# Attention on eight 64-by-32 tiles of the array, a batch at a time, and PReLU as one scaling and one maximum

## The chip, the core and the metric

The program runs on one core of one Trainium2 chip. Its engines work side by side: TensorE (PE; its weight loads are listed apart as PEld), VectorE (DVE), ScalarE (ACT), GpSimd (POOL) and SyncE (SP), whose queue issues the transfers between HBM and the on-chip memory SBUF. TensorE writes to PSUM, in banks of 128 partitions by 512 words. Each engine works through its own list in order. The metric is the time of one execution in microseconds (us); three runs of the kernel before took 1742.65, 1750.32 and 1750.9 us, median 1750.32.

## The reference, cut to what matters

Eight batches, eight heads, 576 tokens of 64 numbers. Attention runs twice through 32 packed rows p of each head, then come two layers over 4608 tokens:

```
p_packed = sm_attn(p, k, v)               # per head: 32 x 576 logits, softmax over 576
x = sm_attn(q, p_packed, p_packed)        # per head: 576 x 32 logits, softmax over 32
h = x @ w_in                              # 512 -> 2048
g = max(h, 0) + alpha * min(h, 0)         # alpha = rand(2048) * 0.3, one for each column
x1 = g @ w_out                            # 2048 -> 512
out = (silu(x1 @ w_gate) * (x1 @ w_val)) @ w_out2     # 512 -> 1536 -> 512
```

The weights arrive as 64-bit floats.

## The kernel before

**Stages.** The first layer runs as 256 units `it`: 16 halves of a batch (288 tokens) by 16 blocks of 128 columns. `h_unit` makes h in six matmuls: the second attention's weights, as a high part and a rest (`a2h`, `a2l`), meet p_packed @ w_in (`ppw`), which `pp_win` has made before, so x itself is never formed. Then PReLU makes `g`, ACT rounds it to `hi` (L773), POOL makes the rest `lo` (L775), and two units later (`LAG1 = 2`) `o_unit` adds twelve matmuls to four banks `acc`. h has two banks. The second layer (L946 on, 72 steps of `gv_step`) follows the last unit.

**Attention.** `quad(g)` handles four heads, two quads to a batch. The 32 packed rows of its four heads fill 128 partitions, and two heads share a matmul: p stands in a block layout with zeros (`pbd`, `ppbd`), so that a matmul uses all 128 rows of the array and 64 columns; a pair `pr` of such matmuls covers the quad. `logits` (L427) does this for both attentions (`s1` with k, `s2` with q), `pp_win` (L579) for p_packed @ w_in, four pieces j to a batch. These matmuls read 32-bit floats and leave two records each in the trace. All other large ones read the format fp32r and leave one.

**PReLU.** Up to unit 47 (`RELU`) ACT makes relu(h) and relu(-h) (L756, L757) and DVE joins them (L758). From unit 48 DVE makes alpha * min(h, 0) and adds max(h, 0) (L762, L765), both from PSUM.

**What sets the order.** `START` and `EARLY` place the steps of batches 0 and 1 (quads a to d) and the conversions of the 32 weight pieces (the word `1`: `convert`, which calls `widen`: four or five DVE instructions, and some of ACT and POOL) before or after a unit. `STEPS`, `GROUPS` and `PPW` do it for batches 2 to 7. From unit 40 to about 240 the weights of the second layer are converted in between (`columns2`, `product2`, `rows2`), and written to HBM over SP's queue. A scheduler that simulates the engines makes the final lists.

Of the kernel before, what the change touches and what calls it, by code (L numbers as in the profile page):

```python
# [17 lines left out]
P = 128  # L18
T = 384
WP = 4  # L20
LAG1 = 2
RELU = 48
# [4 lines left out]
LOADS = "b.v a.v 1 a.q 1 1 b.q"  # L27
START = """
    a.kt0 b.kt0 a.pt a.kt1 b.kt1 b.pt a.s1 a.et a.pp b.s1 a.ppt b.et b.qt0 a.qt0 b.pp b.qt1 a.qt1
    a.s20 b.ppt b.s20 a.a20 b.a20 1 1 1 1 1 w00 1 1  # L30
"""
EARLY = {
    (0, 0): "c.pd d.pd",
    (0, 1): "c.pt 1 b.s21 c.kt0 c.kt1",
    (1, 0): "c.s1",
    (1, 1): "d.kt0 d.pt 1 c.et d.qt0 c.pp",
    (2, 0): "c.qt0",
    (3, 0): "w01 d.qt1 a.s21",
    (3, 1): "c.ppt b.a21",
    (4, 1): "1 d.kt1 d.s1 a.a21 c.qt1",  # L40
    (5, 1): "1",
    (6, 1): "1 d.et",
    (7, 0): "d.pp",
    (7, 1): "1",
    (10, 1): "c.s2 d.ppt d.s2 w10",
    (11, 1): "1",
    (13, 0): "d.a2",
    (15, 0): "c.a2",
# [20 lines left out]
BEHIND = {"c.k": 3, "c.q": 4, "c.v": 5, "d.k": 5, "d.q": 6, "d.v": 9}  # L69
# [6 lines left out]
    p=0, k=0, v=2, kt0=0, pt=1, kt1=3.5, s1=3.5, q=0, et=4.5, pp=6.5, qt0=4, qt1=10.5, ppt=7,  # L76
    s2=11, a2=15,
)
GROUPS = (4, 9.5)
# [25 lines left out]
def tile_kernel(  # L105
# [20 lines left out]

    nc = tc.nc
# [7 lines left out]
    HQ = 4  # L135
# [5 lines left out]
    NQ = H // HQ  # L141
# [38 lines left out]
    def col_job(w, table, name, f):  # L180


        def parts():
            c = slice((f % WP) * P, (f % WP + 1) * P)
            return [t[:, :, c] for t in piece(table, f // WP, name)]

        return w[:, 2 * f * P : 2 * (f + 1) * P].rearrange("(c p) f -> p c f", p=P), parts

    def row_job(w, table, name, f):


        def parts():
            return [t[:, f % WP, :] for t in piece(table, f // WP, name)]

        return w[f * P : (f + 1) * P, :], parts
# [60 lines left out]
    def convert(n=1):  # L256

        for src, parts in queue[:n]:
# [17 lines left out]
    def vscratch(name):  # L276
        return vp.tile([P, HQ * M6 * D], U32, tag="v", name=name)

# [17 lines left out]
    pbd = sm.tile([P, P], F32, name="pbd")  # L296
    ppbd = [sm.tile([P, P], F32, name=f"ppbd{i}") for i in range(2)]
    for t in [pbd] + ppbd:
        nc.vector.memset(t, 0.0)
    al = sm.tile([P, NF1], F32, name="al")  # L300
    nal = sm.tile([P, NF1], F32, name="nal")
# [3 lines left out]
    def quad(g, ptags=("at",), natural=False, evac=nc.scalar):  # L305


        b, q2 = divmod(g, NQ)
        h0 = HQ * q2
        st = {"t": 0}  # L310
        wide = nc.gpsimd if g == 3 else nc.vector

        def pst(shape, name):
            tag = ptags[st["t"] % len(ptags)]
            st["t"] += 1
            return ps.tile(shape, F32, tag=tag, name=f"{name}_{g}", bufs=2)

        def alloc(name):
            return utile("u", [P, S], f"{name}_{g}")

        def copy(out, in_):

            if evac is nc.scalar:
                nc.scalar.activation(out=out, in_=in_, func=AF.Copy)
            else:
                evac.tensor_copy(out=out, in_=in_)

        def load_t(src, name, perm):
            tiles = []
            for pr in range(2):  # L330
                t = alloc(f"{name}{pr}")
                for hh in range(2):
                    s = src[b, h0 + 2 * pr + hh]
                    for e in range(2):
                        blk = 2 * hh + e
                        dst = t[32 * blk : 32 * blk + 32, :]
                        if perm:
                            nc.sync.dma_start(
                                out=dst.rearrange("p (m u i) -> p m u i", i=32, m=M6),
                                in_=s.rearrange(  # L340
                                    "(u j m) (e i) -> e j m u i", j=32, m=M6, i=32
                                )[e],
                            )
                        else:
                            nc.sync.dma_start(
                                out=dst.rearrange("p (t i) -> p t i", i=32),
                                in_=s.rearrange("(t j) (e i) -> e j t i", j=32, i=32)[e],
                            )
                tiles.append(t)
            return tiles  # L350

        def s_p():
            st["pb"] = pbd
            for h in range(HQ):
                nc.sync.dma_start(
                    out=pbd[32 * h : 32 * h + 32, (h % 2) * D : (h % 2) * D + D],
                    in_=p[b, h0 + h],
                )

        def s_p_dense(pd, pb):  # L360
            st["pb"] = pb
            for h in range(HQ):
                nc.gpsimd.tensor_copy(
                    out=pb[32 * h : 32 * h + 32, (h % 2) * D : (h % 2) * D + D],
                    in_=pd[32 * h : 32 * h + 32, :],
                )

        def load_n(src, name):

            if natural:  # L370
                t = wflat("B", f"{name}_{g}")
            else:
                t = vp.tile([P, HQ * M6 * D], F32, tag="v", name=f"{name}_{g}")
            t = t[:PB, : HQ * M6 * D].rearrange("p (h m d) -> p h m d", h=HQ, m=M6)
            nc.sync.dma_start(
                out=t.rearrange("p h m d -> p h (m d)"),
                in_=src[b, h0 : h0 + HQ].rearrange("h (p m) d -> p h (m d)", p=PB),
            )
            return t

        def s_v():
            st["v"] = load_n(v, "v")

        def s_k():
            st["kr"] = load_n(k, "k") if natural else load_t(k, "kr", True)

        def s_q():
            st["qr"] = load_n(q, "q") if natural else load_t(q, "qr", False)

        def s_kt(pr):  # L390
            t = alloc(f"kT{pr}")
            st.setdefault("kT", []).append(t)
            if not natural:
                nc.vector.transpose(out=t, in_=st["kr"][pr])
                return
            turn(t, st["kr"], pr, "kt", "q (i e p) -> q e i p")

        def turn(t, src, pr, name, order):

            for h in range(2):  # L400
                tp = pst([P, 512], f"{name}{pr}{h}")
                flat = src[:, 2 * pr + h].rearrange("p m d -> p (m d)")
                for i in range(M6 // 2):
                    nc.tensor.transpose(
                        tp[:, i * PB : (i + 1) * PB], flat[:, i * P : (i + 1) * P], ident[:PB, :PB]
                    )
                for e in range(2):
                    copy(
# [687 lines left out]
```

## Time and profile before

| | |
|---|---|
| median of three runs | 1750.32 us |
| profiled execution | 1746.27 us, its span 1744.5 us |
| busy share of the span | PE 95%, PEld 85%, DVE 58%, POOL 46%, ACT 35% |
| mean granted TensorE clock | 0.985 |
| chain that ended last | PE 79%, DVE 8%, DMA 4%, issue 3% |

How to read it: a busy time is that of an engine's instructions; matmuls overlap in their pipeline, so the step from one matmul's start to the next is what it costs. Three stretches differ: the start (to about 235 us), the rest of the first layer (to 881 us), and the second layer.

### The profile page before, as it was taken

The numbers are of one execution on the slowest core, as the hardware profiler recorded it, in microseconds if no ns is written. First come the engines' busy times: TensorE is split into PE (matmuls) and PEld (weight loads), VectorE is DVE, ScalarE is ACT, GpSimd is POOL, SyncE is SP. The second block draws the span as 40 slices with busy tenths as digits, with TensorE's granted clock in tenths as the row PEclk, the third lists the DMA queues.
The fourth block names the chain that finished last, engine by engine and source line by source line (L and its number), as shares of the span: only waits on it lengthen the run. The fifth ranks groups of instructions, "written<-read, shape, count | busy, mean of one in ns | idle before, by whom it ended". The sixth has DMA issues, their size and how long they took to land.

```text
span 1744.5 us, 27383 instructions
## 1 busy us (share of the span) xinstructions
PE 1664.1 (95%) x10048; PEld 1476.3 (85%) x10048; DVE 1011.9 (58%) x1875; ACT 611.4 (35%) x1384; POOL 807.9 (46%) x824
## 2 busy tenths in 40 slices
PE   5698899999999999999999999999999999999997
PEld 3477687978888798988999989989988998999997
DVE  6999867686777768675553363363354336334332
ACT  6765553433344344342222232232232223223222
POOL 3556755656555555533333443433433434433443
PEclk7799999999999999999999999999999999999999
DMA  9433365554545445431264464445455446445442
GB/s 237 123 97 107 113 181 155 145 133 135 152 131 152 127 129 145 120 113 57 80 243 167 169 203 165 169 165 204 169 185 184 157 145 226 161 145 193 172 169 79
DMA packets 227749, 266.03 MB, mean 153 GB/s; under 512 B 130848, under 2 KB 190240, under 8 KB 227616
## 3 DMA queue, kind: packets, MB, share of 16 engines
q1 hardware_dynamic: 227616, 264.30, 47.7%
q8 instruction: 79, 1.29, 0.3%
q14 instruction: 54, 0.44, 0.1%
HBM read 214.70 MB, written 49.55 MB: 151 GB/s over the span
## 4 chain that ended last, share of the span: by engine, by line
PE 79%; DVE 8%; DMA 4%; issue 3%; ACT 2%; POOL 2%; SPq 1%; ACTq 0%; DVEq 0%; POOLq 0%
PE acc L290 6%; PE acc L292 6%; PE acc L291 6%; PE o L291 6%; PE o L292 6%; PE o L290 5%; PE yb L290 4%; PE yb L291 4%; PE yb L292 4%; PE h L290 3%; PE h L292 3%; PE h L291 3%; PE vb L291 3%; PE xb L291 3%; PE vb L292 3%
## 5 line engine op out<-in xcount | busy, mean ns | idle before, releaser
L775 POOL TENSOR_TENSOR lo<-g,hi 128x288 fp32r<-128x288 f32 x256 | 222.3, 871 | 230.3 <-ACT hi L773 192.4
L979 POOL TENSOR_TENSOR s<-s,p 128x384 f32<-128x384 f32 x72 | 74.5, 1034 | 475.1 <-ACT s L978 475.1
L773 ACT ACTIVATE hi<-g 128x288 fp32r<-128x288 f32 x256 | 112.3, 441 | 240.9 <-DVE g L765 166.2
L940 DVE TENSOR_TENSOR u<-vb,u 128x384 f32<-128x384 f32 x144 | 80.2, 557 | 186.2 <-PE vb L292 185.9
L292 PE MATMUL o<-wp,ph 128*128 128x512 f32 x432 | 171.9, 398 | 0.0
L291 PE MATMUL o<-wp,ph 128*128 128x512 f32 x432 | 171.3, 396 | 0.0
L290 PE MATMUL h<-a2h,ppw 128*128 128x288 f32 x512 | 159.2, 311 | 10.9 <-DVE ppw L590 4.9
L290 PE MATMUL o<-wp,pl 128*128 128x512 f32 x432 | 168.5, 390 | 1.0 <-POOL pl L1001 1.0
L762 DVE TENSOR_SCALAR g<-h,al 128x288 f32<-128x288 f32 x208 | 105.5, 508 | 103.4 <-PE h L292 80.7
L940 DVE TENSOR_TENSOR u<-yb,p 128x384 f32<-128x384 f32 x144 | 79.4, 551 | 146.7 <-PE yb L292 146.7
L290 PE MATMUL yb<-ring,gv 128*128 128x384 f32 x432 | 146.0, 338 | 7.6 <-DVE u L940 7.2
L292 PE MATMUL h<-a2l,ppw 128*128 128x288 f32 x512 | 152.0, 297 | 0.0
L291 PE MATMUL h<-a2h,ppw 128*128 128x288 f32 x512 | 152.0, 297 | 0.0
L1001 POOL TENSOR_TENSOR pl<-s,ph 128x384 fp32r<-128x384 f32 x144 | 146.8, 1038 | 5.8 <-ACT ph L999 5.8
L292 PE MATMUL yb<-ring,gv 128*128 128x384 f32 x432 | 144.4, 334 | 0.0
L291 PE MATMUL yb<-ring,gv 128*128 128x384 f32 x432 | 144.4, 334 | 0.0
L978 ACT ACTIVATE s<-p 128x384 f32<-128x384 f32 x72 | 37.7, 524 | 287.7 <-DVE p L940 287.7
L290 PEld LDWEIGHTS h<-a2h,ppw 128*128 128x128 f32 x512 | 97.3, 190 | 41.5 <-DVE g L765 10.8
L999 ACT ACTIVATE ph<-s 128x384 fp32r<-128x384 f32 x144 | 75.7, 526 | 138.5 <-DVE s L983 116.7
L985 POOL TENSOR_TENSOR s<-s,u 128x384 f32<-128x384 f32 x72 | 102.4, 1423 | 5.5
L290 PE MATMUL xb<-ring,gv 128*128 128x384 f32 x288 | 97.2, 338 | 6.9 <-DVE u L940 6.9
L966 DVE TENSOR_TENSOR s<-xb,s 128x384 f32<-128x384 f32 x72 | 40.0, 556 | 106.2 <-ACT s L965 106.2
(176 smaller groups left out, 4685.3 us busy)
## 6 DMA issues: line engine op xcount, KB each, us to landing
gv<-wgvd SPq DMA_DIRECT2D x144, 896.0 KB, 6.3
wgvd<-cva SPq DMA_DIRECT2D x84, 256.0 KB, 2.7
cva<-in_moe_w_out_dram SPq DMA_DIRECT2D x28, 512.0 KB, 3.5
v<-in_v_dram SPq DMA_DIRECT2D x16, 576.0 KB, 6.0
out_dram<-os SPq DMA_DIRECT2D x12, 768.0 KB, 3.9
cva<-in_moe_w_in_dram SPq DMA_DIRECT2D x16, 512.0 KB, 3.7
kr<-in_k_dram SPq DMA_DIRECT2D x96, 72.0 KB, 2.7
qr<-in_q_dram SPq DMA_DIRECT2D x96, 72.0 KB, 2.4
```

The costliest lines, as they stand in the source:

```text
L290: nc.tensor.matmul(o, wlo, xhi, start=start, stop=False, **kw)
L291: nc.tensor.matmul(o, whi, xhi, start=False, stop=False, **kw)
L292: return nc.tensor.matmul(o, whi, xlo, start=False, stop=stop, **kw)
L762: nc.vector.tensor_scalar(out=g32, in0=hp, scalar1=0.0, scalar2=al[:, f : f + 1], op0=ALU.min, op1=ALU.mult)
L773: nc.scalar.activation(out=hi, in_=x, func=AF.Copy)
L775: nc.gpsimd.tensor_tensor(out=lo, in0=x, in1=f32(hi), op=ALU.subtract)
L940: nc.vector.tensor_tensor(out=out, in0=bank, in1=x, op=ALU.add)
L966: nc.vector.tensor_tensor(out=s1, in0=xb, in1=s1, op=ALU.mult)
L979: nc.gpsimd.tensor_tensor(out=s2, in0=s2, in1=p1, op=ALU.mult)
L985: nc.gpsimd.tensor_tensor(out=s2, in0=s2, in1=u3, op=ALU.mult)
L999: nc.scalar.activation(out=hi, in_=x, func=AF.Copy)
L1001: nc.gpsimd.tensor_tensor(out=lo, in0=x, in1=f32(hi), op=ALU.subtract)
```

## The change

A batch is now one step (`attention(b)`), with all eight heads in it. Head 2i+r uses rows 64r to 64r+63 of the array and columns 32i to 32i+31. The zeros go, and so do the block layouts. What was a pair of matmuls for each of two quads is one set of eight smaller ones (`heads8`), whose results lie in two banks. The products with v use four tiles of 32 columns and 64 moving columns instead of two of 64 and 128. For batches 0 and 1, k and q are turned by plain 32-bit matmuls instead of transposes, and copied out 128 partitions at once. The first logits are copied to SBUF by ACT before their maximum. PReLU becomes one ACT instruction and one of DVE; rows of w_out get the sign `sg` (1 for alpha up to 1) in one more ACT instruction for each piece. `START`, `EARLY`, `STEPS` and `BEHIND` are rewritten; `GROUPS` goes.

```
+    def heads8(out, lhs, rhs):
+        for i in range(HP):
+            for r in range(2):
+                rows, n = slice(64 * r, 64 * r + 64), slice(32 * i, 32 * i + 32)
+                nc.tensor.matmul(out[r][n], lhs[rows, n], rhs[i][rows], start=True, stop=True)
...
-            for pr in range(2):          # logits: one bank, two matmuls
-                nc.tensor.matmul(t[64 * pr : 64 * pr + 64, :HS], lhs[:, 64 * pr : 64 * pr + 64],
-                    rhs[pr][:, half * HS : (half + 1) * HS], start=True, stop=True)
+            t = [pst(f"{name}{half}{r}")[:, :HS] for r in range(2)]
+            heads8(t, lhs, [rhs[i][:, c] for i in range(HP)])
...
+            for half in range(2):        # s_s1
+                s1 = logits(st["pT"], st["kT"], half, "s1")
+                for r in range(2):
+                    nc.scalar.activation(
+                        out=e[r][:, half * HS : (half + 1) * HS], in_=s1[r], func=AF.Copy)
...
+            for m in range(M6):          # s_pp
+                for i in range(HP):
+                    c = (m % 4) * P + 32 * i
+                    nc.tensor.matmul(pp[32 * i : 32 * i + 32, :D],
+                        st["ET"][r][m // 4][:PB, c : c + 32], v_of(r, i, m),
+                        start=(m == 0), stop=(m == M6 - 1))
...
-        for q2 in range(NQ):             # pp_win
-            for pr in range(2):
-                nc.tensor.matmul(o[r, :], ppT[NQ * b + q2][:, r], w[:, 2 * q2 + pr, :], ...)
+        heads8(o, ppT[b], [w[:, i, :] for i in range(HP)])
...
-        if it < RELU:                    # h_unit
-            begun[it] = nc.scalar.activation(out=r, in_=hp, func=AF.Relu)
-            nc.scalar.activation(out=g32, in_=hp, func=AF.Relu, scale=-1.0)
-            nc.vector.scalar_tensor_tensor(out=g32, in0=g32, scalar=nal[:, f : f + 1], in1=r, ...)
-        else:
-            nc.vector.tensor_scalar(out=g32, in0=hp, scalar1=0.0, scalar2=al[:, f : f + 1], ...)
-            nc.vector.scalar_tensor_tensor(out=g32, in0=hp, scalar=0.0, in1=g32, ...)
+        begun[it] = nc.scalar.activation(out=m, in_=hp, func=AF.Copy, scale=sal[:, f : f + 1])
+        nc.vector.scalar_tensor_tensor(
+            out=g32, in0=hp, scalar=sg[:, f : f + 1], in1=m, op0=ALU.mult, op1=ALU.max)
...
+                nc.scalar.activation(out=full, in_=full, func=AF.Copy, scale=sg[:, f : f + 1])
...
+STEPS = dict(
+    p=4, k0=4, k1=4, kt0=4, k2=4, kt1=5, k3=5, kt2=6, kt3=7, v0=4, pt=5, s1=8, et0=9.5, et1=11,
...
```

Before, on TensorE at unit 122, where piece 0 of batch 4's product with w_in is made (`ppw_00` and `ppw_01` are the banks of the two quads; x2 is the pair of a quad):

```order
L291 MATMUL acc_112_5262<-hi_5421,wo1h 128x288
L292 MATMUL acc_112_5262<-lo_5423,wo1h 128x288
L586 MATMUL ppw_00_5696<-wi_124,ppT_4957 64x512 x2
L586 MATMUL ppw_01_5701<-wi_124,ppT_5180 64x512 x2
L290 MATMUL h_5519<-a2h_4052,ppw_2_4218 128x288
L291 MATMUL h_5519<-a2h_4052,ppw_2_4218 128x288
```

After the change, at the same unit (`ppw_00` and `ppw_01` are now the banks of r = 0 and 1):

```order
L288 MATMUL acc_112_5496<-hi_5653,wo1h 128x288
L289 MATMUL acc_112_5496<-lo_5655,wo1h 128x288
L306 MATMUL ppw_00_5930<-wi_115,ppT_5350 32x512 x4
L306 MATMUL ppw_01_5931<-wi_115,ppT_5350 32x512 x4
L287 MATMUL h_5747<-a2h_3_4315,ppw_2_4389 128x288
L288 MATMUL h_5747<-a2h_3_4315,ppw_2_4389 128x288
```

Four matmuls of 64 columns have become eight of 32, at the same place. Not everywhere do the eight stand together. Piece 2 of batch 5, after the change, on TensorE about unit 150:

```order
L288 MATMUL acc_144_6785<-hi_6800,wo0h 128x288
L289 MATMUL acc_144_6785<-lo_6802,wo0h 128x288
L306 MATMUL ppw_20_6956<-wi_1527,ppT_6639 32x512
L306 MATMUL ppw_21_6957<-wi_1527,ppT_6639 32x512
L287 MATMUL h_6895<-a2h_4_5598,ppw_1_6045 128x288
L288 MATMUL h_6895<-a2h_4_5598,ppw_1_6045 128x288
L289 MATMUL h_6895<-a2l_4_5599,ppw_1_6045 128x288
```

Here two of the eight stand alone; the other six come 36 matmuls later. On ScalarE, before, at units 120 to 123:

```order
L773 ACTIVATE hi_5461<-g_120_5458 128x288
L702 ACTIVATE cva_103<-cva_102 128x256
L562 ACTIVATE a2h_5469<-a_5471 128x576
L773 ACTIVATE hi_5500<-g_121_5497 128x288
L589 ACTIVATE ppw_0_5695<-ppw_00_5696 128x512
L589 ACTIVATE ppw_0_5695<-ppw_01_5701 128x512
L773 ACTIVATE hi_5529<-g_122_5526 128x288
L773 ACTIVATE hi_5567<-g_123_5564 128x288
```

And after, at units 122 and 123 (`m` is sal * h, read from PSUM; `cva` are second-layer weights, L688 is L702 of before):

```order
L576 ACTIVATE ppw_0_5929<-ppw_01_5931 128x512
L735 ACTIVATE m_5755<-h_5747,sal 128x288
L688 ACTIVATE cva_100<-cva_100 128x256
L735 ACTIVATE m_5794<-h_5786,sal 128x288
L746 ACTIVATE hi_5758<-g_122_5754 128x288
L688 ACTIVATE cva_100<-cva_100 128x256
L746 ACTIVATE hi_5797<-g_123_5793 128x288
```

The first reading of h, which was DVE's, now stands in ACT's list, among the weight conversions.

## Rows read from the trace of the kernel before

**Rows 1.** Windows of the three stretches: us, then each engine's busy us (instructions).

```profile
0.00:235.00 235.00, 186.77 (x1178) 144.87 (x1179) 203.88 (x337) 144.98 (x344) 142.56 (x142) 0.91 0.50 135
235.00:881.00 646.00, 637.17 (x4528) 557.60 (x4527) 455.46 (x925) 244.66 (x587) 332.80 (x383) 1.00 0.47 132
881.00:1744.00 863.00, 840.13 (x4347) 773.79 (x4345) 352.55 (x614) 221.76 (x454) 332.56 (x299) 0.99 0.48 173
```

**Rows 2.** The same view, one stretch of the start: PE, PEld, DVE, ACT, POOL.

```profile
100.00:150.00 50.00, 45.04 (x319) 38.00 (x319) 46.63 (x76) 31.14 (x77) 32.12 (x29) 1.00 0.40 108
```

**Rows 3.** Timeline of PE, both column tiles at work: start, us, instruction, count.

```profile
510.15 0.30 PE L292 MATMUL h<-a2l,ppw 128*128 128x288 f32 x1
510.38 1.19 PE L430 MATMUL s<-kT,pT 128*64 128x288 f32 x8
511.50 0.40 PE L290 MATMUL acc<-hi,wo0l 128*128 128x288 f32 x1
511.74 0.29 PE L291 MATMUL acc<-hi,wo0h 128*128 128x288 f32 x1
511.86 0.29 PE L290 MATMUL h<-a2h,ppw 128*128 128x288 f32 x1
```

**Rows 4.** Timeline of PE, two matmuls of one and the same column tile.

```profile
567.27 0.29 PE L290 MATMUL h<-a2h,ppw 128*128 128x288 f32 x1
567.49 1.19 PE L430 MATMUL s<-qT,ppT 128*64 128x288 f32 x4
568.61 0.40 PE L291 MATMUL h<-a2h,ppw 128*128 128x288 f32 x1
```

**Rows 5.** Chain in order of time: start, us, line, records.

```profile
581.89 1.01 PE ppw L586 x4
...
630.90 1.87 PE ppw L586 x8
636.03 1.46 PE pp L492 x24
642.89 0.64 PE s L430 x4
```

**Rows 6.** Groups by line and shape on PE, 235 to 881 us.

```profile
L586 PE MATMUL ppw<-wi,ppT 128*64 128x512 f32 x192 | 48.9, 608 | 0.6 <-DVE ppw L590 0.6
...
L430 PE MATMUL s<-qT,ppT 128*64 128x288 f32 x96 | 23.6, 420 | 0.1
```

**Rows 7.** Groups by line and shape on DVE, 0 to 220 us.

```profile
L758 DVE SCALAR_TENSOR_TENSOR g<-g,nal,r 128x288 f32<-128x288 f32 x39 | 33.4, 856 | 6.2 <-ACT g L757 6.0
...
L326 DVE COPY qT<-qt 64x288 f32<-64x288 f32 x8 | 5.4, 676 | 1.1 <-PE qt L404 0.9
...
L326 DVE COPY kT<-kt 64x288 f32<-64x288 f32 x8 | 3.6, 455 | 9.3 <-PE kt L404 9.2
```

**Rows 8.** PReLU lines one by one: count, shortest/median/longest ns, first and last start.

```profile
L758 DVE SCALAR_TENSOR_TENSOR g<-g,nal,r x48: 502/560/1573, 60.1 to 244.7; 128x288 f32<-128x288 f32 x48
...
L762 DVE TENSOR_SCALAR g<-h,al x208: 411/512/521, 248.3 to 879.9; 128x288 f32<-128x288 f32 x104
...
L765 DVE SCALAR_TENSOR_TENSOR g<-h,g x208: 410/456/460, 249.3 to 880.4; 128x288 f32<-128x288 f32 x104
...
L756 ACT ACTIVATE r<-h x48: 388/395/413, 57.4 to 243.9; 128x288 f32<-128x288 f32 x48
```

**Rows 9.** Timelines of DVE and of POOL near 74 us.

```profile
74.02 1.55 DVE L758 SCALAR_TENSOR_TENSOR g<-g,nal,r 128x288 f32<-128x288 f32 x1
...
73.85 1.41 POOL L252 TENSOR_TENSOR wi<-cva,cva 128x512 f32<-128x512 f32 x1 [2.10 <-DVE cva L242]
```

**Rows 10.** Waits, 250 to 880 us: who, for whom, us in total, times, longest.

```profile
ACT cva L702 <- DMA wgvd<-cva: 43.7, 31, 3.5
...
ACT cva L215 <- DMA cva<-in_moe_w_val_dram: 16.1, 10, 5.0
...
ACT cva L712 <- DMA wgvd<-cva: 13.1, 6, 3.8
...
PEld h L290 <- DVE g L765: 10.8, 14, 2.2
```

More of the change, by code (lines that the diff above doesn't have):

```diff
@@ L295, in tile_kernel @@
     make_identity(nc, ident)
[L296 to L299, printed above, removed]
+    ppd = [sm.tile([P, P], F32, name=f"ppd{i}") for i in range(2)]
     al = sm.tile([P, NF1], F32, name="al")
-    nal = sm.tile([P, NF1], F32, name="nal")
+    sg = sm.tile([P, NF1], F32, name="sg")
+    sal = sm.tile([P, NF1], F32, name="sal")
     spare = sm.tile([P, 1], F32, name="spare")
@@ L395, in s_kt @@
                 return
[L396 to L408, printed above, removed]
-                        t[D * h : D * h + D, :].rearrange(order, e=2, p=PB)[:, e],
-                        tp[D * e : D * e + D, :HS].rearrange("q (i p) -> q i p", p=PB),
-                    )
+            src = st[name][i // 2][:, 2 * (i % 2) : 2 * (i % 2) + 2]
@@ new lines, in s_turn @@
+            order = dict(k="q (m p) -> q m p", q="q (p m) -> q m p")[name]
+            for e in range(2):
+                tp = pst(f"{name}t{i}{e}")
+                for m in range(M6 // 2):
+                    for r in range(2):
+                        nc.tensor.matmul(
+                            tp[D * r : D * r + D, m * PB : (m + 1) * PB],
+                            src[:, r, 3 * e + m, :],
+                            ident[:PB, :PB],
+                            start=True,
+                            stop=True,
+                        )
+                out = t.rearrange(order, m=M6)[:, 3 * e : 3 * e + 3]
+                in_ = tp[:, :HS].rearrange("q (m p) -> q m p", m=M6 // 2)
+                if evac[i % 2] is nc.scalar:
+                    nc.scalar.activation(out=out, in_=in_, func=AF.Copy)
+                else:
+                    evac[i % 2].tensor_copy(out=out, in_=in_)
@@ L437, in logits @@
             return t
         def s_s1():
-            s1 = [logits(st["pT"], st["kT"], half, "s1") for half in range(2)]
-            mx = sm.tile([P, 4], F32, tag="mx", name=f"mx_{g}")
-            for half in range(2):
-                nc.vector.tensor_reduce(
-                    out=mx[:, half : half + 1], in_=s1[half][:, :HS], axis=AX.X, op=ALU.max
-                )
-            nc.vector.tensor_reduce(out=mx[:, 2:3], in_=mx[:, 0:2], axis=AX.X, op=ALU.max)
-            nc.vector.tensor_scalar_mul(mx[:, 3:4], mx[:, 2:3], -SCALE)
@@ L467, in s_s1 @@
-            nc.vector.reciprocal(out=sums[:, 3:4], in_=sums[:, 2:3])
+            if b == 1:
+                both = wflat("B", "E_1")
+                e = [both[:, r * S : (r + 1) * S] for r in range(2)]
+                both = wflat("B", "ET_1")
+                st["ET1"] = [both[:, r * 1024 : r * 1024 + 768] for r in range(2)]
+            else:
+                e = [alloc(f"E{r}") for r in range(2)]
+            for half in range(2):
+                s1 = logits(st["pT"], st["kT"], half, "s1")
+                for r in range(2):
+                    nc.scalar.activation(
+                        out=e[r][:, half * HS : (half + 1) * HS], in_=s1[r], func=AF.Copy
+                    )
@@ new lines, in s_s1 @@
+            mx = sm.tile([P, 4], F32, tag="mx", name=f"mx_{b}")
+            for r in range(2):
+                nc.vector.tensor_reduce(out=mx[:, r : r + 1], in_=e[r], axis=AX.X, op=ALU.max)
+            nc.vector.tensor_scalar_mul(mx[:, 2:4], mx[:, 0:2], -SCALE)
+            sums = sm.tile([P, 6], F32, tag="sums", name=f"sums_{b}", bufs=2)
+            for r in range(2):
+                nc.scalar.activation(
+                    out=e[r],
+                    in_=e[r],
+                    func=AF.Exp,
+                    bias=mx[:, 2 + r : 3 + r],
+                    scale=SCALE,
+                    accum_out=sums[:, r : r + 1],
+                )
@@ L515, in s_s2, with spans @@
+        def spans(halves):
             n = len(halves) * HS
             lo = halves[0] * HS
[L517 to L526 removed]
```

453 lines of the change are left out of this document (197 added, 256 removed).

## The prediction

> **What bounds the kernel now.** I read the windows first, then the timeline of TensorE, then groups, single lines and waits. The windows split the first layer in two. From 235 to 881 us PE is busy 637 of 646 us: whatever its matmuls give up there comes off the time, as long as no other engine is late. Up to 235 us PE is busy 187 us only, and DVE 204; between 100 and 150 us DVE is busy 46.6 of 50 us, ahead of PE (45.0), POOL and ACT [rows 1, 2]. There DVE's work sets the pace. The second layer, 863 us, holds none of the changed code.
>
> So two prices are wanted: a visit of TensorE to attention work, and DVE's work per unit.
>
> **What the tiles cost now.** In the timeline, matmuls of 288 columns in fp32r start 0.13 us apart (511.74, 511.86). Logits come at 510.38; the first matmul after them starts 1.12 us later, and the gaps on both sides (510.15 to 510.38, 511.50 to 511.74) are 0.10 and 0.11 us longer than 0.13 [rows 3]. That visit was four matmuls, two on each column tile, eight records. The visit at 567.49 takes 1.12 us too, with four records, two matmuls of one column tile alone [rows 4]. Half the work in the same time: the two column tiles run side by side, and what costs is the number of turns on the fullest tile, not of matmuls. From the chain: a visit with one pair of logits 0.64 us, with two 1.12, so a turn (one matmul on each tile) is 0.48 us; a pair of 512 columns 1.01 us, two 1.87, so a turn is 0.86; six turns of the product with v 1.46 us, 0.22 a turn [rows 3, 5]. What is left of each visit (0.64 - 0.48, and so on), with the two longer gaps, is 0.35 us: the price of leaving and regaining the full array.
>
> **The change on TensorE, 235 to 881 us.** I counted turns and visits in the two orders from unit 37 on.
> - p_packed @ w_in: before, 192 records are 48 pairs [rows 6]; with two that stand before 235 us, 50 turns by 0.86 = 43.0 us. After: 24 pieces would be 24 turns, but the order splits some (two, then six), and a part costs a whole turn: 39. Eight tiles start one behind the other; I add 0.05 us a turn. 39 x 0.91 = 35.5. Gain 7.5.
> - Logits: before 66 turns by 0.48 = 31.7. After 33, by 0.53 = 17.5. Gain 14.2.
> - Products with v: before 72 turns by 0.22 = 15.6. After 72 turns with 64 moving columns instead of 128 on four tiles. No row shows such a short one: between half (0.11, if columns set it) and the same (0.22). I take 0.125, near the half, since the 0.48 and 0.86 turns go with their columns (288 : 512); 9.0. Gain 6.6, bounds 0 and 7.7.
> - Visits: 87 of this kind become 84. Gain 1.
> - Transposes of p: 24 become 12, of 128 columns and one record each, so not above the 0.13 us of rows 3. Gain 1.
>
> Sum 30 us, bounds 24 and 31. It rests on one thing that no row shows: that four column tiles by two row tiles run side by side like two column tiles do.
>
> The Trainium skill ("TensorE: Matmul & The Clock Gate", Measured speedup vs the span model) speaks against full credit: it states 2.38 for three tiles and 6.32 for nine, about 0.7 of ideal at nine. At 0.7 a turn of logits would be about 0.69 us and one of 512 columns 1.23, and the sum 18 us less, an estimate from that page. With two tiles, rows 3 and 4 show no such loss.
>
> **The change on DVE, up to 235 us.** L758 joins the two halves of PReLU from SBUF: 39 times by 220 us, 856 ns on average, 33.4 us [rows 7]. Its times are of two kinds, 502 at best, 560 in the middle, 1573 at worst [rows 8]. At 74.02 one takes 1.55 us while POOL runs an addition from 73.85 to 75.26 [rows 9]. L765, which reads PSUM and one tile of SBUF, has 410 to 460 ns in 208 cases, L762 at most 521 [rows 8], beside POOL work of 333 in 646 us [rows 1]. The new instruction has L765's form, so 0.46. Gain 39 x (0.856 - 0.456) = 15.6 us.
> The Trainium skill ("SBUF — State Buffer", two separate sides) names the cause: a port pair that DVE, with two SBUF inputs, and GpSimd lock in turn. The trace agrees in the 1.55 us; by it POOL gains too, of which I count nothing.
> The copies L326 (5.4 + 3.6 us [rows 7]) become 8 of 128 partitions at the same length, gain 4.5; maxima and sums in fewer, longer instructions, about 2. Together 22 us of DVE's work. Against it: PE's turning of batches 0 and 1 becomes plain matmuls of two records, some 8 us more (96 pairs of 96 columns, 0.48 x 96/288 = 0.16 us each, in place of 96 transposes of a single record, which I take at half); the first chain (k, logits, copies, exp, products) must now carry eight heads before anything of the second attention starts; sixteen pieces get one more ACT instruction; and the order puts more conversions ahead of unit 0. When DVE gives up 22 us, PE (187 of 235 us busy, at a mean granted clock of 0.91 [rows 1]) is close behind it. I count 12 of the 22; bounds +3 (nothing won, the longer chain shows) and -24.
>
> **After unit 48** DVE drops one instruction of 0.51 us for each of 208 units, ACT gains one of about 0.40 (L756's price [rows 8]), some 83 us on 245 busy of 646 [rows 1]. Neither engine bounds there. But m now stands in ACT's list behind conversions that wait for transfers: 43.7, 16.1 and 13.1 us of such waits, 5.0 us the longest [rows 10]. Until now h's bank was freed by DVE, which had no such waits. From the end of h's matmuls to the next use of the bank lie about 4 us (two units of 18 matmuls by 0.13 less h's own 0.8); m, g and two handovers need 1. A wait under 3 us costs nothing. The bounds are -11 (the 10.8 us that weight loads waited for g go [rows 10]) and +73 (every wait on a transfer reaches PE); I take 3, near the lower end, since the waits of the largest group average 1.4 us.
>
> **Sum.** 1746.3 (the profiled execution, 1744.5 of it the span) - 30 - 12 + 3 = 1707. That execution stands 4 us under the median of the runs shown, 1750.3, and 3.6 over the lowest; I leave 1707.
>
> **Rivals.**
> 1. *Eight tiles side by side are slower than two*: their operands come from more places at once, and each turn costs a third more. The 72 turns are 17.5 + 35.5 = 53 us, a third is 18: 1725. For it: rows 3 have two tiles, none has eight; against it: two cost no more than one [rows 3, 4]. 0.15. (The page named above would have it so.)
> 2. *Row tiles do not run side by side*, only column tiles do: each set of eight is two turns. 33 + 39 sets get a second one, 17.5 + 35.5 = 53 us: PE gives back all and 23 more; with the start's 12 won the time is about 1760. Nothing in this trace uses two row tiles. 0.05.
> 3. *ACT's list becomes the wait.* m queues behind transfers, h's bank comes free late, PE stands. In all, waits on transfers are some 73 us; more than half of it (42 us) must reach PE to eat the gain, which needs waits mostly over 3 us, while the group of 31 averages 1.4. In full: 1707 + 70 = 1777; in part (20 us) 1727. 0.10, of which 0.02 for slower than before.
> 4. *The start gives everything*, 24 us or more, because POOL too is freed of the lock: 1695. 0.20.
> 5. *The start gives nothing*, since transfers and the first chain set it, not DVE: 1719 to 1722. 0.10.
> My forecast keeps 0.40.
>
> **How the numbers follow.** Rivals 1, 4, 5 and the mild form of 3 lie at 1695 to 1727; with the bounds of the forecast (1707 - 14, 1707 + 18) and the 4 us between execution and median, the range is 1684 to 1736. A difference below 0.5% (9 us) can't be told from none. Faster by more than that, under 1741: all but rival 2, the hard end of 3 and some of 1 with 5 together, 0.88. Same 0.07, slower 0.05.
>
> **What would show it.** The changed profile should have logits visits of eight matmuls at about 0.7 us from first start to the next full matmul, and 512-column ones at about 1.1, where now a pair takes 0.64 and 1.01. If 1.1 and 1.9 stand there, rival 2 holds. The product with v: 12 turns in about 0.8 to 0.9 us a visit. The new DVE instruction: below 0.5 us everywhere, without the 1.5 us kind. Unit 40 should start some 12 us earlier, the second layer some 40 us earlier, and last the same 863 us. The forecast is wrong if PE's idle time before h, with ACT's m as its releaser, grows past 10 us, or if the start is no shorter.

## The result, and the profile after

The changed kernel takes 1772.28 us (median of 4 runs), the kernel before 1748.93 beside it: ratio 1.0145, interval [1.0125, 1.0164]. Forecast were 1707 us, in 1684 to 1736. It is slower by 1.45%, and the forecast is wrong in its sign.

Where it goes is read from windows cut at the same work: the first matmul of h of unit 40, and that of unit 255. Columns as in [rows 1]; the last three are granted clock, DMA share and GB/s. The kernel before:

```profile
0.00:219.70 219.70, 171.83 (x1058) 131.01 (x1059) 193.23 (x314) 133.93 (x312) 130.30 (x128) 0.91 0.49 136
219.70:878.80 659.10, 649.91 (x4632) 569.26 (x4630) 465.14 (x945) 255.44 (x619) 344.25 (x396) 1.00 0.47 131
878.80:1744.50 865.70, 842.33 (x4364) 776.00 (x4362) 353.52 (x616) 222.03 (x455) 333.36 (x300) 0.99 0.48 173
```

The changed kernel:

```profile
0.00:240.20 240.20, 176.76 (x1574) 138.67 (x1574) 174.89 (x288) 118.60 (x250) 127.33 (x111) 0.80 0.48 127
240.20:904.00 663.80, 628.10 (x5286) 549.88 (x5283) 383.26 (x683) 328.65 (x768) 346.03 (x395) 0.99 0.47 129
904.00:1774.00 870.00, 844.61 (x4364) 778.68 (x4362) 352.30 (x615) 222.54 (x456) 332.74 (x300) 0.99 0.48 173
```

Unit 40 starts 20.5 us later, where I forecast 12 earlier. The middle stretch is 4.7 us longer, where I forecast 27 shorter: TensorE's busy time did fall there, by 21.8 us, but its idle time rose from 9.2 to 35.7. The second layer is 4.3 us longer here; over the runs below, which leave it alone, it takes 860.3 to 873.0 us. The two profiled executions lie 29.5 us apart and the medians 23.4: the profile of the changed kernel is its slowest run.

The tiles themselves do what they should. TensorE's timeline of the changed kernel (start, us, instruction, records) has a whole set of logits, a part of a set of 512 columns, a whole such set, and a product with v:

```profile
452.62 0.71 PE L306 MATMUL s<-kT,pT 64*32 64x288 f32 x16
453.26 0.40 PE L287 MATMUL acc<-hi,wo1l 128*128 128x288 f32 x1
...
627.80 1.04 PE L306 MATMUL ppw<-wi,ppT 64*32 64x512 f32 x2
628.77 0.40 PE L287 MATMUL h<-a2h,ppw 128*128 128x288 f32 x1
...
661.43 1.09 PE L306 MATMUL ppw<-wi,ppT 64*32 64x512 f32 x16
662.45 0.40 PE L288 MATMUL acc<-hi,wo2h 128*128 128x288 f32 x1
...
478.43 0.88 PE L470 MATMUL pp<-v,ET 96*32 96x64 f32 x48 [1.50 <-DMA v<-in_v_dram]
```

Eight matmuls of 288 columns take 0.64 us to the next full matmul (0.65 in most sets), where one pair took 0.64 before [rows 5]; eight of 512 take 1.02 (a pair 1.01 before [rows 5]). One matmul of such a set alone takes 0.97. The last line has a wait that the kernel before did not have.

The costliest group of the new PReLU on each of DVE and ACT (busy, mean ns | idle before, what ended it), where before stood [rows 7, 8]:

```profile
L738 DVE SCALAR_TENSOR_TENSOR g<-h,sg,m 128x288 f32<-128x288 f32 x256 | 129.3, 508 | 172.9 <-ACT m L735 160.1
...
L735 ACT ACTIVATE m<-h,sal 128x288 f32<-128x288 f32 x256 | 125.3, 494 | 64.8 <-PE h L289 64.6
```

DVE's instruction is 0.51 us (0.46 forecast) and never over 0.52, m 0.49 (0.40 forecast). And the waits from 240 to 904 us (who, for whom: us in total, times, longest), as [rows 10]:

```profile
DVE g L738 <- ACT m L735: 146.4, 87, 4.3
...
PEld h L287 <- DVE g L738: 27.2, 32, 2.0
DVE qT L372 <- DMA qr<-in_q_dram: 25.4, 16, 3.7
...
PEld acc L289 <- POOL lo L748: 11.6, 21, 1.2
...
PE h L287 <- DVE g L738: 9.1, 13, 1.7
...
PE pp L470 <- DMA v<-in_v_dram: 8.5, 5, 3.4
```

Weight loads of h wait 27.2 us for g, not 10.8 [rows 10]. The forecast had named two signs against it. PE's idle time before h with m as its releaser did not pass 10 us: it is 9.1 us, and the releaser is g, though g in its turn waits 146.4 us for m. The other sign is there: the start is no shorter. The waits for transfers of q and of v are new too: the kernel before has none on v there, and 1.3 us on q.

To add TensorE up, I took every matmul's time to the next one's start, between units 40 and 255. Matmuls of the attention: 111.8 us before, 89.8 after, so 22.0 saved of the 30 forecast. The 3870 full-array matmuls, the same number in both: 547.3 us before, 574.0 after, so 26.7 more. The second number eats the first. Sorted by what comes next on TensorE, 13.1 of the 26.7 stand right ahead of attention matmuls (v's 8.5 us among them), 11.0 ahead of matmuls of acc, and 3.1 ahead of those of h.

### The profile page after: what moved, and what is told of

Same layout as the page of the kernel before. It is cut to its first block, busy times and chain, and to the rows that moved or that the text cites. A ratio compares the mean times of both kernels' runs of the same rounds, so it can differ in the third digit from the quotient of the medians.

```text
span 1774.0 us, 29492 instructions
## 1 busy us (share of the span) xinstructions
PE 1649.5 (93%) x11216; PEld 1467.2 (83%) x11216; DVE 910.5 (51%) x1585; ACT 669.8 (38%) x1472; POOL 806.1 (45%) x806
## 4 chain that ended last, share of the span: by engine, by line
PE 61%; issue 9%; POOL 9%; DMA 9%; DVE 8%; ACT 2%; SPq 2%; POOLq 0%; DVEq 0%; ACTq 0%
PE o L288 5%; PE o L289 5%; PE o L287 5%; PE yb L287 4%; PE yb L289 4%; PE yb L288 4%; POOL lo L748 3%; PE acc L289 3%; PE acc L287 3%; PE acc L288 3%; DMA wgvd<-cva 3%; PE vb L288 3%; PE xb L288 3%; PE vb L289 3%; PE vb L287 3%
## 5 line engine op out<-in xcount | busy, mean ns | idle before, releaser
L738 DVE SCALAR_TENSOR_TENSOR g<-h,sg,m 128x288 f32<-128x288 f32 x256 | 129.3, 508 | 172.9 <-ACT m L735 160.1
L287 PE MATMUL h<-a2h,ppw 128*128 128x288 f32 x512 | 161.7, 316 | 24.8 <-DVE g L738 17.4
L913 DVE TENSOR_TENSOR u<-vb,u 128x384 f32<-128x384 f32 x144 | 80.2, 557 | 187.2 <-PE vb L289 187.0
L288 PE MATMUL h<-a2h,ppw 128*128 128x288 f32 x512 | 154.1, 301 | 0.0
L735 ACT ACTIVATE m<-h,sal 128x288 f32<-128x288 f32 x256 | 125.3, 494 | 64.8 <-PE h L289 64.6
L289 PEld LDWEIGHTS h<-a2l,ppw 128*128 128x128 f32 x512 | 98.6, 193 | 7.8 <-issue 4.8
```

Of the source, the lines that this page charges most:

```text
L287: nc.tensor.matmul(o, wlo, xhi, start=start, stop=False, **kw)
L288: nc.tensor.matmul(o, whi, xhi, start=False, stop=False, **kw)
L289: return nc.tensor.matmul(o, whi, xlo, start=False, stop=stop, **kw)
L735: begun[it] = nc.scalar.activation(out=m, in_=hp, func=AF.Copy, scale=sal[:, f : f + 1])
L738: nc.vector.scalar_tensor_tensor(out=g32, in0=hp, scalar=sg[:, f : f + 1], in1=m, op0=ALU.mult, op1=ALU.max)
L913: nc.vector.tensor_tensor(out=out, in0=bank, in1=x, op=ALU.add)
```

## The experiments

All times are medians; each ratio is to the kernel before in the same session. "Unit 40" is its start, "40 to 255" the stretch between these two starts, both from the profiled execution.

| run | us | ratio, interval | unit 40 | 40 to 255 |
|---|---|---|---|---|
| before | 1748.93 | | 219.7 | 659.1 |
| after | 1772.28 | 1.0145 [1.0125, 1.0164] | 240.2 | 663.8 |
| e1 tiles, old PReLU | 1800.21 | 1.0305 [1.0282, 1.0329] | 257.5 | 672.8 |
| e2 new PReLU alone | 1749.23 | 1.0009 [0.9997, 1.0022] | 217.5 | 657.6 |
| e3 tiles from batch 2, old PReLU | 1771.22 | 1.0124 [1.0098, 1.0151] | 222.2 | 676.5 |
| e4 start reordered | 1775.23 | 1.0153 [1.0134, 1.0171] | 236.0 | 663.9 |
| e5 later use | 1780.17 | 1.0165 [1.0134, 1.0195] | 244.2 | 671.2 |
| e6 tiles from batch 2, new PReLU | 1763.81 | 1.0079 [1.0063, 1.0095] | 217.9 | 673.9 |
| e7 e6 with later use | 1760.65 | 1.0067 [1.0049, 1.0085] | 218.8 | 669.5 |
| e8 before, late q | 1750.00 | 1.0010 [0.9996, 1.0025] | 222.2 | 657.0 |
| e9 one v | 1773.10 | 1.0151 [1.0120, 1.0182] | 236.3 | 662.5 |
| e10 no q loads | 1760.11 | 1.0081 [1.0054, 1.0107] | 240.2 | 658.1 |
| e11 both | 1756.40 | 1.0058 [1.0038, 1.0078] | 241.1 | 650.8 |
| e12 spread loads | 1763.66 | 1.0104 [1.0078, 1.0129] | 238.2 | 654.3 |
| e13 e12, whole sets | 1788.37 | 1.0232 [1.0213, 1.0250] | 245.7 | 672.3 |
| e14 e12, third unit | 1755.55 | 1.0048 [1.0030, 1.0067] | 238.6 | 644.7 |
| e15 e6, spread, whole sets | 1762.30 | 1.0093 [1.0060, 1.0125] | 215.9 | 674.5 |
| e16 e2, less TensorE work | 1732.42 | 0.9916 [0.9899, 0.9932] | 216.1 | 641.9 |
| e17 e6, spread, third unit | 1744.31 | 0.9970 [0.9956, 0.9984] | 225.0 | 652.7 |
| e18 e2, third unit | 1751.45 | 1.0016 [1.0005, 1.0027] | 220.9 | 660.8 |

**The two halves of the change, apart: e1, e2, e3.** My first theory was that m in ACT's list had eaten the tiles' gain (theory A).

```diff
 # e1 on the changed kernel; e2 is the reverse, on the kernel before; e3: `if b < 2` old attention, else tiles
-        m = gp.tile(...); nc.scalar.activation(out=m, in_=hp, func=AF.Copy, scale=sal[:, f : f + 1])
-        nc.vector.scalar_tensor_tensor(out=g32, in0=hp, scalar=sg[:, f : f + 1], in1=m, op0=ALU.mult, op1=ALU.max)
+        if it < RELU: ...   # ACT twice, DVE once
+        else: ...           # DVE twice
```

> The changed kernel with the PReLU of before (ACT's two steps up to unit 47, two DVE instructions after it; w_out not scaled, no sg). Theory A: in the changed kernel m stands in ACT's list behind work that waits, g waits for m, and h's bank comes free late; that ate the 30 us which the tiles save. Then units 40 to 255 take 664 - 28 = about 636 us here, weight loads of h wait for g under 15 us (61 us of idle there in the changed kernel), and the time is about 1742. Rival B: the attention itself lost them (late transfers of v and q, more copies on ACT); then units 40 to 255 still take 655 to 665 us and the time is 1765 to 1772. The start stays late in both: unit 40 at 235 to 240 us.

> The kernel before with the new PReLU alone (m on ACT, one DVE instruction, rows of w_out scaled by ACT), attention untouched. Theory A: units 40 to 255 grow from 659 to about 680 us, with DVE's g waiting for ACT's m and h's weight loads for g; the start gains a few us at most; time 1760 to 1772. Rival B: the new PReLU costs nothing on the old attention; units 40 to 255 stay at 659, the start gains up to 12 us; time 1738 to 1750.

> The kernel before with its own start (batches 0 and 1 in the old attention) and its own PReLU; eight tiles only for batches 2 to 7. Theory A: the tiles give their 24 to 30 us when the PReLU is left as it was: units 40 to 255 take about 632 us, unit 40 starts where it did before (220 us), time about 1720. Rival B: the tiled attention brings waits of its own (v and q transfers, its longer chain): units 40 to 255 take 645 to 660 us, time 1735 to 1748.

Theory A falls on all three. The new PReLU alone changes nothing (1.0009), though DVE's g waits 161 us for m in that run too. With the tiles, the old PReLU is 28 us slower than the new one, 17 of them before unit 40. And tiles alone lengthen the middle stretch by 17 us (e3). Both e1 and e3 are worse than rival B had them, too. So the loss sits with the tiled attention, and the new PReLU softens it. DVE's groups up to unit 40, in the changed kernel, in e1 and in e2:

```profile
L738 DVE SCALAR_TENSOR_TENSOR g<-h,sg,m 128x288 f32<-128x288 f32 x39 | 19.5, 505 | 14.8 <-ACT m L735 11.8 <-POOL cva L689 2.7 <-POOL wi L248 0.2
```

```profile
L733 DVE SCALAR_TENSOR_TENSOR g<-g,nal,r 128x288 f32<-128x288 f32 x39 | 30.3, 778 | 16.5 <-ACT g L732 16.4
```

```profile
L765 DVE SCALAR_TENSOR_TENSOR g<-h,sg,m 128x288 f32<-128x288 f32 x39 | 19.7, 506 | 10.2 <-ACT m L762 6.3 <-POOL lo L775 2.1 <-POOL cva L710 1.8
```

The instruction fell from 856 ns [rows 7] to 506 in e2 as forecast, 13.7 us in 39 units; unit 40 came 2.2 us earlier (unit 0 starts 1.9 us later, units 0 to 39 take 4.1 us less). Little of DVE's time was what the old start waited for.

**The start: e4, e6.**

```diff
 # e4 on the changed kernel; in START three conversions move behind the first logits
-LOADS = "a.v0 a.v1 1", "a.q0 1 1 a.q1"
+LOADS = "a.v0 a.v1 a.q0 a.q1"      # alpha's load ahead of them; conversions 0 to 2 held behind the first Exp
 # e6: the kernel before up to batch 1, with the new PReLU; attention(b) and pp_win on tiles for b >= 2
```

> The changed kernel with its start in another order: alpha and q are loaded ahead of the first weights, and the first three conversions and sg are held until the maximum and the Exp of the first attention. Theory C: the first chain was late because kT's and E's copies stood behind conversions that wait for transfers; then unit 0 starts at about 68 us (80 in the changed kernel), unit 40 some 8 to 12 us earlier (about 230), time about 1762. Rival D: conversions set unit 40 whatever the chain does; unit 0 moves by a few us, unit 40 stays at 238 to 245, time 1770 to 1776.

> The start and the first two batches of the kernel before, eight tiles for batches 2 to 7 only, and the new PReLU. If the start's loss and the loss after unit 40 are separate sums, unit 40 starts near 217 us as with the new PReLU alone, units 40 to 255 take about 664 us as in the changed kernel, and the time is about 1750. Rival: the late start of the changed kernel is also what delays the later units (weight pieces converted later); then units 40 to 255 take 640 us or less, time about 1725.

The changed kernel's longest waits of TensorE up to 240 us, and the chain followed back from 82 us, by line:

```profile
PE et L456 <- ACT E L438: 13.8, 2, 10.7
PE h L287 <- DVE g L738: 8.3, 6, 2.5
PE h L287 <- ACT a2h L543: 7.3, 1, 7.3
...
by line: DMA cva<-in_moe_w_in_dram 18.8%; issue 9.9%; DMA cva<-in_moe_w_out_dram 9.1%; SPq L349 9.0%; DMA k<-in_k_dram 6.3%; DVE cva L231 5.7%; DVE cva L238 4.0%; DVE cvb L212 3.9%; DVE cva L223 3.0%; DVE cvb L223 2.9%; POOL cva L236 2.6%; 
```

The first chain carries eight heads and stands in ACT's and DVE's lists between conversions that wait for weights. Unit 0 starts at 80.2 us instead of 50.9. All of the start's loss lies before it: units 0 to 39 take 160.0 us, 8.8 less than before. With the chain put first (e4) unit 0 starts at 71.4, but unit 40 gains only 4 us and the time nothing: the first seven pieces of w_out came 5 to 11 us later instead. With the old start (e6) unit 40 is back at 217.9. So the start's 20 us belong to the first two batches on tiles, with the order that was written for them. The middle stretch of e6, though, takes 673.9 us and not 664, so the time is 1764 and not the 1750 expected; its TensorE visits to p_packed @ w_in take 52.5 us instead of 45.2. Why, I could not settle; the order of its instructions differs.

**Transfers of q and v: e5, e7, e8.** In eight rotating buffers now stand the tiles of eight heads, and v's two halves share one buffer. The changed kernel's timeline shows q's transfers and v's second half issued in one stretch, and DVE and TensorE waiting:

```profile
471.30 1.91 SPq L336 DMA_DIRECT2D qr<-in_q_dram  x2
472.03 0.78 DVE L372 STREAM_TRANSPOSE qT<-qr 128x576 f32<-128x576 f32 x1 [0.28 <-DMA qr<-in_q_dram]
...
473.31 0.44 SPq L349 DMA_DIRECT2D v<-in_v_dram  x1
473.80 5.33 SPq L336 DMA_DIRECT2D qr<-in_q_dram  x7
474.34 0.78 DVE L372 STREAM_TRANSPOSE qT<-qr 128x576 f32<-128x576 f32 x1 [1.53 <-DMA qr<-in_q_dram]
475.04 0.48 DVE L738 SCALAR_TENSOR_TENSOR g<-h,sg,m 128x288 f32<-128x288 f32 x1
...
479.54 0.78 DVE L372 STREAM_TRANSPOSE qT<-qr 128x576 f32<-128x576 f32 x1 [2.52 <-DMA qr<-in_q_dram]
480.24 0.48 DVE L738 SCALAR_TENSOR_TENSOR g<-h,sg,m 128x288 f32<-128x288 f32 x1
```

After the second and the third turn of q comes a g whose m had been ready for 2.2 and 2.4 us.

```diff
 # e5, e7
-    ... qt0=12, q2=12, qt1=13, q3=13, pp1=15, qt2=15, qt3=16, ppt=15.5, s2=18, a2=22,
+    ... q2=11.5, q3=12, qt0=13.5, qt1=14.5, pp1=16, qt2=16.5, qt3=17.5, ppt=16.5, s2=19.5, a2=23.5,
 # e8, on the kernel before
-    ... q=0, et=4.5, pp=6.5, qt0=4, ...
+    ... et=4.5, q=4.5, pp=6.5, qt0=5, ...
```

> The changed kernel with more units between a transfer and its use, by the table of steps alone: q's last two loads up to 1 unit earlier, turning of q 1.5 units later, the second product with v 1 unit later, what follows 1 to 1.5 units later. Theory E: the tiled attention holds eight heads' tiles at once in eight buffers, so q and v come late; DVE stands at qT for q's transfers (25 us in the changed kernel), and g, behind it in DVE's list, frees h's bank late. Then that wait falls under 10 us, h's weight loads wait for g under 40 us of idle (61), units 40 to 255 take 638 to 650 us (664), time about 1750 to 1760. Rival F: the wait for q is covered, and the loss lies elsewhere (m on ACT, copies in ACT's list, larger lumps of TensorE work); then the wait falls, and units 40 to 255 still take 658 to 666 us, time 1768 to 1774.

> The kernel of the run with the old start and the new PReLU, with the table of steps that leaves more units between transfer and use. Theory E: 12 to 25 us less than that run without the new table, so 1725 to 1738, faster than both kernels. Rival F: within 5 us of it, about 1750.

> The kernel before, with q loaded half a unit ahead of its turning instead of four units, nothing else. Theory E: DVE now waits for q's transfers there too, 20 to 40 us over 12 groups of four heads, h's weight loads wait for g more than the 10.8 us of before, and the time is 1757 to 1772. Rival F: the wait appears and costs under 5 us, time 1745 to 1753.

e5 and e7 did not test what they were meant to: DVE still waits 29.1 and 27.3 us for q, since q's loads wait for their buffers and moved along. They moved the middle stretch by +7 and -4 us, which says how much a new order alone can do. In e8 DVE waits 13.1 us for q and 16.5 for k (1.3 and 5.9 before), and the time stays, as rival F had it: with the old attention waits of this size are covered. At 13.1 us for q it is half of the changed kernel's wait, and less than the 20 to 40 that it was built for.

**Taking the transfers away: e9 to e12.**

```diff
 # e9: v_of returns st["v"][0] for both halves, v loaded once a batch
 # e10: q's tile is loaded once, for batch 2, into a tile of its own; UBUFS u=8 -> 7. e11: both
 # e12, all of the work kept: E's turned tiles are taken right after E
+                if not natural:
+                    st["ETs"] = [[alloc(f"ET{r}{i}") for i in range(2)] for r in range(2)]
-    ... s1=8, et0=9.5, et1=11, q0=11, q1=11, pp0=11.5, v1=11.5, qt0=12, q2=12, qt1=13, q3=13, ...
+    ... s1=8, q0=8.5, q1=8.5, et0=9.5, q2=10, et1=11, pp0=11.5, v1=11.5, q3=12, qt0=13, qt1=14, ...
```

> The changed kernel without the second load of v in batches 2 to 7: both products read the first one (the output is not attention's; every matmul stays). Theory G: v's one buffer and the burst of q's and v's transfers make the second product wait (gaps ahead of pp 8.5 us, and 10.0 us ahead of its visits against 1.2 before); then the gaps ahead of pp go under 1.5 us, and units 40 to 255 take 653 to 657 us (664), time about 1763. Rival H: pp's wait covers other waits that come instead; units 40 to 255 stay within 3 us of 664.

> The changed kernel with q loaded once into a tile of its own and turned from there for all of batches 2 to 7 (the output is not attention's); seven rotating buffers stay for the rest. It takes away DVE's 25 us of waiting for q's transfers, and 96 small-packet transfers less 4. Theory G: g's behind qT come earlier, v's transfer has the queues to itself; units 40 to 255 take 648 to 655 us, time 1757 to 1764. Rival H (lumps of copies and reductions in ACT's and DVE's lists, not transfers, delay g, m and hi): h's and acc's gaps stay at 20 us together, units 40 to 255 at 658 or more.

> Both of these together: q never loaded again, v once a batch. Theory G: nearly all that ate the gain after unit 40 goes; units 40 to 255 take 638 to 648 us, and the full-array matmuls' time over 0.1217 us each falls from 103 us to 80 to 88 (76 before). Rival H: 655 us or more.

> The changed kernel with the same work and buffers and its loads spread: the tiles of the turned exponentials are taken before q's first two, so that those are loaded right after the first logits, the third after the first turn of exponentials, and v's second half stands ahead of q's last in SP's queue; turning of q 1 unit later. If the burst is the cause, DVE's wait for q falls from 25 us to under 8, pp's gaps from 8.5 to under 3, units 40 to 255 take 645 to 655 us and the time is 1753 to 1765. If not the waits move to other places and the time stays at 1768 to 1776.

v's wait alone was covered by others (e9: 1.3 us; rival H was right there). Without q's loads 5.7 us go, without both 13.0: less than theory G had. (In e11's text 103 and 76 us are the 574.0 and 547.3 from above less 0.1217 us for each of the 3870 matmuls; that is a subtrahend and no spacing, the shortest in the traces being 0.125. By it e11 has 89.5.) Spread out, with nothing left out, the loads give 9.5 us of the stretch, as expected, and the ratio falls from 1.0145 to 1.0104. In e12's waits, 240 to 890 us, q's are down from 25.4 to 4.0, v's stay (under 3 was expected), and lo's have grown:

```profile
PEld acc L289 <- POOL lo L750: 16.1, 21, 2.1
...
PEld h L287 <- DVE g L740: 11.7, 18, 1.1
...
PE acc L289 <- POOL lo L750: 9.2, 15, 1.8
...
PE pp L472 <- DMA v<-in_v_dram: 7.7, 5, 2.7
...
DVE qT L372 <- DMA qr<-in_q_dram: 4.0, 3, 1.5
```

By the sum of matmuls, the 9.5 us come off the attention (89.8 to 80.9); the full-array matmuls keep their 26 us (573.3).

**What is left: e13, e14, e16, e18.** Theory S: with less attention on TensorE, two units no longer cover the chain m, g, hi, lo with the delays in ACT's and POOL's lists.

```diff
 # e14 on e12, e18 on e2
-LAG1 = 2
+LAG1 = 3
 # e13 on e12: in a set, tc.keep_in_program_order(mm); the ten products after it issue behind it; steps up to 1 unit later
 # e16 on e2: batches 2 to 7
-            for pr in range(2):
+            for pr in range(2 if b < 2 or q2 == 0 else 0):
```

> The run with spread loads, and TensorE's order pinned so that the eight matmuls of a set stand together (24 visits for p_packed @ w_in in batches 2 to 7 instead of 42, 12 for the first logits instead of 16; halves of the logits 1 unit apart). A part of a set takes as long as a whole one (0.97 to 1.02 us), so about 20 visits at 1.0 us and 0.3 us around them fall away. If TensorE's own time still decides, units 40 to 255 take 630 to 640 us (654), time about 1742. If the other engines' chain (m, g, hi, lo) decides once TensorE has less to do (theory S), gaps ahead of acc and h grow instead, and units 40 to 255 stay at 648 or more.

> The run with spread loads, and one more unit between a unit's h and its second product (three in place of two; one more buffer each of hi and lo, bought by sharing two small tiles). Theory S: with less attention work on TensorE a unit is shorter, and two units no longer cover m, g, hi and lo with the delays in ACT's and POOL's lists; then the gaps ahead of acc (13.2 us) and weight loads of acc waiting for lo (16.1 us) go under 4 us each, and units 40 to 255 take 640 to 646 us (654). Otherwise the waits are for h's bank alone, and the length stays within 3 us.

> The kernel before with the new PReLU, and in batches 2 to 7 only the first half of p_packed @ w_in is computed and used for both halves (the output is not the reference's); copies on ACT and DVE stay. TensorE loses 24 pairs of matmuls, about 24 x 0.93 = 22 us, with nothing of the tiled attention in the kernel. Theory S: part of what TensorE gives up comes back as waits for g and lo; units 40 to 255 fall by 8 to 15 us (from 658), gaps ahead of h and acc rise from 5 to 10 or more. Rival H (the lumps of the tiled attention make the waits): all 20 to 25 us come off and the gaps stay at 5.

> The kernel before with the new PReLU and three units between h and its second product (one buffer of m, the turned p in a rotating buffer), old attention throughout. Theory S says that two units cover the chain there (gaps ahead of acc 4 us): units 40 to 255 take 652 to 658 us (658), time within 6 us of 1749. If a third unit is worth as much here as with the tiles (10 us), the wait was no matter of TensorE's shorter units; then 645 to 649 us.

e14 takes another 9.6 us, as theory S had it: the gaps ahead of acc fall from 13.2 to 3.7 us, and the weight loads of acc wait 0.9 us for lo instead of 16.1. Some come back ahead of h (2.3 to 9.5). With 644.7 us the middle stretch is now 14.4 us shorter than in the kernel before, about half of the 27 forecast. How much of the 9.6 is the third unit's own is not shown: TensorE's idle time as a whole stays (26.8 and 26.9), and in e14's order p_packed @ w_in stands in 34 parts instead of 42 and takes 6.4 us less. In the old attention the third unit gives nothing (e18: gaps ahead of acc 4.0 to 1.8, but 9.9 instead of 0.7 ahead of h, where m had one buffer less, so the two are not parted). e14's waits, 235 to 890 us:

```profile
PEld h L287 <- DVE g L740: 22.4, 28, 2.4
...
PE h L287 <- DVE g L740: 9.2, 12, 2.1
...
PEld acc L289 <- POOL lo L750: 0.9, 3, 0.5
```

e16 has no tiles at all. Its p_packed @ w_in takes 27.8 us less (57.0 to 29.2, time to the next start), its logits, in another order, 4.7 more; all of its attention takes 23.3 us less, and the stretch is only 15.7 us shorter. Its window, under that of e2:

```profile
217.50:875.10 657.60, 650.83 (x4627) 566.70 (x4627) 386.72 (x732) 340.07 (x813) 344.55 (x395) 1.00 0.48 130
```

```profile
216.10:858.00 641.90, 628.16 (x4533) 565.93 (x4532) 387.65 (x732) 341.61 (x813) 348.21 (x395) 0.99 0.48 133
```

TensorE's idle time doubles, 6.8 to 13.7 us, with every other engine's work nearly unchanged. Neither theory had it exactly: about a third came back, without any lump of tiles. Nor did it come back where theory S looked for it. The waits for g and lo fell, in e2 and then in e16:

```profile
PEld h L291 <- DVE g L765: 11.0, 16, 0.8
...
PEld acc L293 <- POOL lo L775: 6.1, 10, 1.2
```

```profile
PEld h L291 <- DVE g L766: 8.7, 11, 2.3
...
PEld acc L293 <- POOL lo L776: 3.8, 7, 0.9
```

Of the 7.4 us that the full-array matmuls take longer in e16, 4.7 stand right ahead of attention matmuls.

e13 shows the other side of the order. All 24 sets stand whole, and the stretch is 18 us longer than in e12: pinned, TensorE waits where it went on with other work before. Its waits, 245 to 918 us:

```profile
PEld h L289 <- DVE g L755: 31.0, 21, 5.6
DVE ppw L593 <- ACT ppw L592: 30.4, 14, 3.8
PEld s L311 <- DVE ppw L593: 25.8, 10, 6.1
```

**Together: e15, e17.** Diffs as above, on e6; e17's third unit is paid for by one buffer of m.

> Old start and first two batches of the kernel before, new PReLU, eight tiles for batches 2 to 7 with spread loads and whole sets. If the start's loss and the losses after unit 40 add up, unit 40 starts near 218 us, the rest takes 640 to 648 us, and the time is 1728 to 1740, faster than both kernels. If the longer visits of that start's kernel stay (its units 40 to 255 took 674 us where the changed kernel took 664), 1745 to 1752.

> Old start and first two batches of the kernel before, new PReLU, eight tiles for batches 2 to 7 with spread loads, and three units between h and its second product (paid for by one buffer of m instead of two, p and its turned form in one tile, and the old attention's turned p in a rotating buffer). If the start's loss and the waits after unit 40 are sums of their own, unit 40 starts at 216 to 224 us, the rest takes 645 to 652 us, time 1732 to 1742, at or under the kernel before. If the old start does not go with it, 1750 or more.

e15 has e13's loss (674.5 us where 640 to 648 were expected). e17 is faster than both kernels, by 0.30% [0.16, 0.44] against the one before, at 1744 us just outside what was expected of it. In its profiled execution, the slowest of its ten, there are 6.4 us less in the middle, and 5.3 more up to unit 40.

```profile
0.00:225.00 225.00, 176.36 (x1054) 133.92 (x1054) 176.48 (x318) 136.16 (x289) 130.25 (x127) 0.88 0.49 131
225.00:877.70 652.70, 620.63 (x5296) 551.04 (x5291) 390.18 (x683) 327.88 (x769) 348.47 (x398) 0.99 0.48 132
```

## Why the prediction was wrong, step by step

- **The price of a turn: right.** Sets of eight cost what a pair cost, to 0.02 us; rivals 1 and 2 are out. The Trainium skill ("TensorE: Matmul & The Clock Gate", Measured speedup vs the span model) states 6.32 for nine tiles. The timeline has 8 x 0.97 / 1.02 = 7.6 for eight, so that loss isn't seen here.
- **The sum of 30 for TensorE: 22.0 measured.** Logits and products with v gave 16.1 and 7.5 (14.2 and 6.6 forecast). p_packed @ w_in gave 1.6 instead of 7.5: 39 visits as counted, but the price was for an undisturbed one, and nine of them took some 6 us more, up to 2.48 us for 1.02, where the second bank came late. The transposes, counted as a small gain, took 3.3 us more.
- **"Whatever its matmuls give up there comes off the time, as long as no other engine is late": the step that failed first.** The condition was stated and then priced at 3 us (bounds -11 and +73); it measured 26.7. I read the 9 us of idle [rows 1] as distance of the other engines. It was not: of the time taken off TensorE about a third came back without tiles (e16), and with tiles 26.7 against 22.0 saved. Rival 3 looked in the wrong place, h's bank behind m in ACT's list: e2 has m there and loses nothing, and only 3.1 of the 26.7 stand ahead of h. What the runs show in its place: loads of q and v that come in one burst (spread in e12, 9.5 us, though off the attention's own time and not off the 26.7), and products of acc that wait for lo, which two units no longer cover (e14, 9.6 us with its new order): 663.8 to 654.3 to 644.7. A new order alone moved the stretch by +7 and -4 us (e5, e7), so the two shares are not sharp.
- **"There DVE's work sets the pace", -12 at the start: the other step that failed.** DVE's work up to unit 40 did fall, from 193.2 to 174.9 us, near the 22 counted. But where it was given its time back alone (e2), unit 40 moved 2.2 us; a busy share of 93% [rows 2] was no proof that others waited for it. Against it stood "the longer chain shows", bounded at +3. It measured 29.3 us at unit 0 and, against e2, 22.7 us at unit 40 (240.2 and 217.5). With this start the new PReLU is worth 17 us (e1), but DVE is busy 77% of units 0 to 39 there, so that its work is the reason is not shown. The granted clock was lower too, 0.80 against 0.91 up to unit 40; how much of the 20 us is its own was not tried.
- **The range.** The bounds given for the three terms add up to 1680 to 1798, which holds the 1772; the range stated, 1684 to 1736, gave the +73 almost no weight. The figures named for it make 1689 to 1731.
- **Open:** why the first chain takes 29 us longer, beyond the conversions between its steps (e4 moved it by 9); some 10 us of the middle stretch of e6; and the rest of the gaps in e14 (26.9 us of idle, 9.2 before).

## What to carry to other kernels

When one engine is busy 98% of a stretch, ask how long the chain on the others is against the time that it has, before crediting a saving in full: take work out of the bound engine and see how much comes off. A wider step (eight heads for four) needs its tiles at once; count buffers and the time between a load's earliest issue and its use, and what stands in the list behind the instruction that waits. A busy engine proves a bound only if someone is seen waiting for it.

## What the runs showed of the hardware that was not expected

A part of a set costs nearly as much as the set: two records of one tile 0.97 us, sixteen of eight tiles 1.02, in one and the same kernel. Eight tiles of 64 rows by 32 columns ran side by side for 0.05 us more than one of them took. An ACT copy with a scale for each partition, read from PSUM, took 494 ns for 288 columns, where the Relu without one took 395 [rows 8]; no run parts the function from the scale.
